# Sliding-window attention and a routed expert layer: loads that wait for units, logits of superchunk 3 from loaded turned values, and routing begun two units sooner

## The chip, the cores and the metric

The kernel runs on one core of a Trainium2 chip. The metric is the device time of the whole kernel in microseconds (us), the median of several runs. Five engines work beside each other, each through its own queue of instructions in order: TensorE (PE, with its weight loads as PEld), VectorE (DVE), ScalarE (ACT), GpSimd (POOL) and SyncE (SP), which here only issues DMAs. They wait for each other by semaphores.

## What is computed

First causal attention with a window of 64 keys, for 8 batches, 8 heads, 576 positions and 64 numbers per head; then, on its output as 4608 rows of 512, a router and eight experts:

```python
scores = scale * np.matmul(q, k.transpose(0, 1, 3, 2))
mask = (rel >= 0) & (rel < window)                      # window = 64
attn = exp(scores - max) / sum                          # per row, under the mask
x = (attn @ v) as (B, S, H * D)
...
logits = np.einsum('bsd,de->bse', x, w_gate)
local_gate = sigmoid(x @ w_local)
e = argmax(logits[b, s]) if s == 0 or local_gate[b, s] < 0.5 else prev_e
h = np.maximum(x[b, s] @ w1[e], 0.0)
out[b, s] = softmax(logits[b, s])[e] * (h @ w2[e])
```

All is in float32. The choice of expert goes along a batch's positions, since a row may take over the expert of the row before.

## The kernel before

**Attention** (function `attention`) takes the 4608 rows in nine superchunks (`sc`, 512 rows each) and each superchunk in four units (`hp`, a pair of heads). A unit's `scores` multiply keys and queries into two banks, ACT takes the exponential into `p` (L416), and VectorE multiplies by the mask (L421), save in the seven units of `BIASED`, where TensorE adds a bias instead. Its `values` (L431) multiply `p` with the values, in two arrangements of the same 512 rows: `va` as loaded and `vb` shifted by half a chunk, which `shift` copies from `va` on ACT and POOL (L360 to L367). A column of ones in the values gives the sum; VectorE takes the reciprocal into `allr` (L436) and multiplies x by it (L441). Scores run two units ahead of values (`LEAD`). After a superchunk POOL writes x to memory (`xs`, L536).

**The gate's logits** come in two ways. For the superchunks in `GATED` (4 to 8) the values turned to columns are loaded (`vtt`), `gates` multiplies them by the gate's weights, and `spread` puts the nine products per head beside the values (`v4`, 74 columns per head in place of 65 in `v3`), so that attention's own product gives the logits (`g`, L439, added up at L534). For the others, 0 to 3, x itself is turned on TensorE in two halves (`turn`, L302, copied by ACT at L305), multiplied and turned back (`gates`, `logits`, L338). The last 64 rows ahead of the first gated superchunk need products too: `gates_ahead` and `back_ahead`.

**Routing** of the first 1728 rows (`Router.first`, `gate`, `places`, `table`) runs beside attention: a generator that is asked for its next piece twice per unit (`step`), each piece saying how long the next should pause, and whether the next one waits for a TensorE result. It begins in unit (4,2), after the logits of superchunk 3. Its end is a table of row numbers by which POOL gathers the first expert's rows.

**Loads.** The queues of TensorE, ACT and SP go in the order of the code; VectorE and POOL are ordered by a scheduler. All loads are issued by SP. Keys and queries of a superchunk (`kq`, 2 MB) lie in a ring of four buffers, v has three buffers and the turned values one. SP issues a load as soon as its buffer is free. Only four times does SP wait for more: `until` issues a copy of one number, and SP waits for that number before it goes on. The first expert's weights, w1 and w2 in four pieces each, go through the same ring.

After attention come the experts: blocks of rows, each two products with an expert's weights, while a second routing for the other rows goes beside the first three. Nothing is changed there.

Of the kernel before, what the change touches and what calls it, by code (L numbers as in the profile page):

```python
# [19 lines left out]
P = 128  # L20
# [22 lines left out]
FB = 3  # L43
# [24 lines left out]
VW = VX + E + 1  # L68
GATED = range(4, NSC)
BIASED = [(4, 3), (5, 1), (5, 3), (6, 0), (6, 1), (6, 2), (6, 3)]  # L70
# [97 lines left out]
def attention(ctx, tc, ring, kq, v3, v4, vt, vh, xs, lt, ok, wg, wg2, ident, rt, ex):  # L168
# [65 lines left out]

    late = cp.tile([1, 4], F32, name="late")

# [113 lines left out]
    def back_ahead():  # L350
        o = bank()[:WIN, :P]
        nc.tensor.transpose(o, ahead, ident)
        nc.scalar.copy(ahead_t[WIN:], o.rearrange("p (h g) -> p h g", h=H)[:, :, :E + 1])

# [69 lines left out]
    def values(sc, hp, p, x, g):  # L424
        va, vb, n = vas[sc], vbs[sc], width(sc)
        xo = pair()
        for s in range(4):
            for j in range(2):
                for par, w in enumerate((vb, va)):
                    b = 2 * s + par  # L430
                    nc.tensor.matmul(xo[par * WIN:(par + 1) * WIN, j, s * VW:s * VW + n],  # L431
                                     lhsT=p[:, j, b * WIN:(b + 1) * WIN], rhs=w[:, s, 2 * hp + j, :n],
                                     start=True, stop=True)
# [7 lines left out]
        nc.vector.tensor_tensor(x[:, :, hp].rearrange("p c j d -> p j c d"), o[:, :, :, :DH],  # L441
                                rr.to_broadcast([P, 2, 4, DH]), op=Alu.mult)

    units = [(sc, hp) for sc in range(NSC) for hp in range(HP)]
    ps = {}
# [25 lines left out]
    for i, (sc, hp) in enumerate(units):  # L471
# [7 lines left out]
        if hp == (0 if sc else 3) and sc + 1 < NSC:  # L479
            moves = shift(sc + 1)  # L480
        for _ in range(2 if sc else 4):
            next(moves, None) if moves else None

        if hp == 3 and sc + 1 in GATED:
            spread(sc + 1, gated)
        elif (sc, hp) == (1, 3):
            gates_ahead()
        elif (sc, hp) == (2, 3):
            back_ahead()
# [27 lines left out]
        if hp == 2 and sc + 1 in GATED:  # L517
            gated = gates(sc + 1)
        if 0 < sc < NSC - 2 and hp == 0:
            load(sc + 2, [whole])  # L520
        if 0 < sc < NSC - 3 and hp == 1:
            load(sc + 3, pairs)
        if hp == 2 and sc + 2 in GATED:
            load(sc + 2, ["turned"])
        if (sc, hp) == (NSC - 3, 3):
            ex.jobs = [ex.weights({}, -1, ("w1",), lambda: until(2, allr[:1, sc, hp, 0, :1]))]
# [175 lines left out]
class Router:  # L702
# [9 lines left out]
    def __init__(self, ctx, tc, lt, xs, tabs, ident):  # L712
        self.nc, self.lt, self.xs, self.tabs, self.ident = tc.nc, lt, xs, tabs, ident
        self.pool = ctx.enter_context(tc.tile_pool(name="rt", bufs=1))
        self.tc, self.behind, self.links = tc, None, []
# [58 lines left out]
    def gate(self, part, psum):  # L774
# [85 lines left out]
        sums = tl("sums", P, 2 * E * CMAX)[:, :2 * n * E]  # L860
        vec.tensor_copy(sums, both)
        pre, tot = sums[:, :n * E], sums[:, n * E:]
# [8 lines left out]
        cnt = self.cnt[part]  # L871
        vec.tensor_tensor(cnt, run[:, :, n - 1], base[:, :, 0], op=Alu.subtract)
        start = tl("start", P, E)
        vec.tensor_copy(start, base[:, :, 0])
        if part:
# [69 lines left out]
    def table(self, psum, cs, ns, lo, hi, idx, gx):  # L945
# [5 lines left out]
        for k in range(0, len(pieces), 2):  # L951
            built = []
            for b, m in pieces[k:k + 2]:
                rowh = self.oh_p.tile([P, PIECE, P], BF16, name="rowh")[:, :m]
                if ns == FIRST:
                    sh = [P, m, P]
                    vec.tensor_tensor(rowh, self.io128.to_broadcast(sh), last(lo[:, b:b + m]).to_broadcast(sh),
                                      op=Alu.is_equal)
                    yield 0.15 * m, False
                one = self.oh_p.tile([P, PIECE, ns], BF16, name="one")[:, :m]  # L960
# [33 lines left out]
    def first(self, psum):  # L994
# [3 lines left out]
        nf = tl("nf", P, E)  # L998
        self.shifted(nf, self.cnt[0], 0, BIG.bit_length() - 1)
        fend = tl("fend", P, E)  # L1000
# [8 lines left out]
        yield 1.8, False  # L1009
        self.experts_of(tabs["ej1"], FB, [(FB, fend)])  # L1010

        CE = [P, C1, E]
        pl = tl("pl", P, CV, E)[:, :C1]
        rank = self.rank[:, :C1]
        vec.tensor_tensor(pl, rank, mid(self.lim1).to_broadcast(CE), op=Alu.is_ge)
        vec.scalar_tensor_tensor(pl, pl, float(2 * N), rank, Alu.mult, Alu.add)
        yield 1.2, False
        vec.tensor_tensor(pl, pl, mid(foff).to_broadcast(CE), op=Alu.add)
        vec.tensor_tensor(pl, pl, self.oh[:, :C1], op=Alu.mult)
        lo, hi = self.places(pl, C1)  # L1020

        vec.tensor_tensor(rank, rank, mid(self.lim1).to_broadcast(CE), op=Alu.subtract)
        yield 2.5, False
        self.weigh(0)
        yield from self.table(psum, slice(0, C1), FIRST, lo, hi, tabs["idx1"], tabs["gx1"])

    def second(self, psum):
# [72 lines left out]
        vec.tensor_tensor(pl, pl, plh, op=Alu.add)  # L1100
        vec.tensor_scalar(none, self.rank[:, :C1], 0.0, float(2 * N), Alu.is_lt, Alu.mult)
        vec.tensor_tensor(pl[:, :C1], pl[:, :C1], none, op=Alu.add)
# [28 lines left out]
class Experts:  # L1131
# [38 lines left out]
    def weights(self, st, n, names=("w1", "w2"), behind=lambda: None):  # L1170
        ej, at = (self.tabs["ej1"], -1 - n) if n < 0 else (self.tabs["ej"], n)
        e = self.nc.values_load(ej[0:1, at:at + 1], engines=[ET.SP], min_val=0, max_val=E - 1,
                                skip_runtime_bounds_check_because="a count of experts, at most E - 1")
        behind()
        for name, w, a, b in (("w1", self.w1, DK, F), ("w2", self.w2, FK, D)):
            if name not in names:
# [6 lines left out]
            st[name] = t.rearrange("p (a b) -> p a b", a=a)  # L1183
        return st

    def begin(self):
# [432 lines left out]
```

## Time and profile before

| what | us |
| --- | --- |
| median of 3 runs (641.36 to 642.15) | 641.81 |
| the profiled execution's own time | 642.1 |
| its span, first to last instruction | 640.0 |
| TensorE busy | 615.6 |
| VectorE busy | 402.3 |
| last value matmul of attention ends | 133.5 |

A stretch is given as start:end in microseconds of the span. A wait in square brackets is the idle time of the engine just ahead of the instruction, and what ended it; "issue" means that nothing in the profile did. A clock of 1.00 is TensorE's full clock. "L431" is line 431 of the kernel before; an x and a number is a count. A float32 matmul of the program is two matmuls, each with a weight load, in the trace.

### The profile page before, as it was taken

Reading aid. Unit: us, or ns where it says so; the run is one execution under the profiler, and the core shown is the slowest. Engines: PE = TensorE matmul, PEld = TensorE weight load, DVE = VectorE, ACT = ScalarE, POOL = GpSimd, SP = SyncE. Lnnn points to the kernel's source line nnn. Section 1 sums busy time; section 2 is a strip of 40 time slices with the busy share of each in tenths; the row PEclk is TensorE's granted clock in tenths of the full one; section 3 lists DMA queues with packets and bytes.
Section 4 is the critical chain, followed back from the end, with each engine's and each line's share of the span. In section 5 each row is a group of like instructions: output and inputs, shape, how many; then the busy total and the mean of one; then the engine's idle time right before and its main releaser. Section 6 shows DMA issues by size and latency. Waiting matters only on the chain. (4 is left out here: it accounts for less than half of the span.)

```text
span 640.0 us, 14994 instructions
## 1 busy us (share of the span) xinstructions
PE 615.6 (96%) x6367; PEld 544.2 (85%) x6367; DVE 402.3 (63%) x752; ACT 200.6 (31%) x368; POOL 133.1 (21%) x132
## 2 busy tenths in 40 slices
PE   8889998899999999999999999999999999999995
PEld 7777777788889999978997999887997998899994
DVE  6676588879968775273654683362917752886730
ACT  3766765612572122113120312021211221213120
POOL 5422112430103202120302120211312022111101
PEclk9999998999999999999999999999999999999998
DMA  9999996969757645786958665769768556956501
GB/s 338 416 418 406 385 366 241 348 236 337 237 171 246 244 166 198 242 316 236 387 189 291 218 234 212 259 235 367 263 228 324 185 199 232 379 167 225 209 17 38
DMA packets 29318, 166.43 MB, mean 260 GB/s; under 512 B 8451, under 2 KB 9497, under 8 KB 20026
## 3 DMA queue, kind: packets, MB, share of 16 engines
q1 hardware_dynamic: 20394, 135.54, 58.4%
q0 software_dynamic: 8848, 29.85, 12.2%
q8 instruction: 52, 0.85, 0.5%
q14 instruction: 24, 0.20, 0.1%
HBM read 146.18 MB, written 19.59 MB: 259 GB/s over the span
## 5 line engine op out<-in xcount | busy, mean ns | idle before, releaser
L1394 POOL DMA_INDIRECT out_dram<-y,idx x36 | 41.1, 1141 | 339.1 <-DVE y L1327 196.5
L1318 PE MATMUL hp<-ws,hs 128*128 128x256 f32 x384 | 88.7, 380 | 0.0
L1318 PEld LDWEIGHTS hp<-ws,hs 128*128 128x128 f32 x384 | 72.6, 190 | 10.5 <-issue 0.8
L1268 PE MATMUL hp<-xs,ws 128*128 128x128 f32 x672 | 79.6, 275 | 0.0
L1268 PEld LDWEIGHTS hp<-xs,ws 128*128 128x128 f32 x672 | 77.3, 192 | 0.0
L1327 DVE SCALAR_TENSOR_TENSOR y<-hp,xg,kept 128x256 f32<-128x256 f32 x48 | 22.6, 482 | 74.2 <-issue 47.0
L1414 PE MATMUL hp<-xt,w 128*64 128x64 f32 (+2 forms) x640 | 66.2, 276 | 0.0
L1414 PEld LDWEIGHTS hp<-xt,w 128*128 128x128 f32 (+1 forms) x640 | 60.8, 170 | 4.1 <-issue 0.7
L1318 PE MATMUL hp<-w,h 128*128 128x256 f32 x256 | 61.1, 382 | 0.0
L1162 POOL DMA_INDIRECT xg<-xs,gx x40 | 50.3, 1258 | 45.6 <-issue 37.4
L1279 DVE TENSOR_TENSOR h<-hp,keep 128x512 f32<-128x512 f32 x42 | 28.6, 690 | 48.1 <-PE hp L1268 48.0
L1268 PEld LDWEIGHTS hp<-xt,w 128*128 128x128 f32 x448 | 53.2, 192 | 2.7 <-issue 1.3
L1268 PE MATMUL hp<-xt,w 128*128 128x128 f32 x448 | 54.7, 275 | 0.0
L1318 PEld LDWEIGHTS hp<-w,h 128*128 128x128 f32 x256 | 47.2, 190 | 6.3 <-issue 0.4
L431 PE MATMUL xo<-vb,p 128*64 128x74 f32 (+1 forms) x576 | 44.5, 230 | 7.0 <-issue 2.9
L416 ACT ACTIVATE p<-sp 128x512 f32<-128x512 f32 x72 | 39.2, 595 | 38.0 <-PE sp L385 35.9
L385 PEld LDWEIGHTS sp<-w 64*64 64x64 f32 x1296 | 38.7, 138 | 12.1 <-issue 8.5
L421 DVE TENSOR_TENSOR p<-p,mask 128x1024 f32<-128x1024 f32 x29 | 36.1, 1245 | 19.5 <-ACT p L416 19.3
L431 PEld LDWEIGHTS xo<-vb,p 128*64 128x64 f32 x576 | 38.9, 138 | 9.9 <-issue 4.4
L385 PE MATMUL sp<-w 64*64 64x128 f32 (+1 forms) x1296 | 43.8, 270 | 2.6 <-issue 1.5
L431 PE MATMUL xo<-va,p 128*64 128x74 f32 (+1 forms) x576 | 44.5, 230 | 1.2 <-issue 1.2
L1280 ACT ACTIVATE h<-h 128x512 f32<-128x512 f32 x42 | 26.3, 630 | 59.1 <-DVE h L1279 59.1
(280 smaller groups left out, 955.0 us busy)
## 6 DMA issues: line engine op xcount, KB each, us to landing
w<-in_w_dram SPq DMA_DIRECT2D x42, 2048.0 KB, 9.2
w<-in_kq_dram SPq DMA_DIRECT2D x17, 1024.0 KB, 8.7
w<-in_w_dram SPq DMA_DIRECT2D x24, 512.0 KB, 9.3
xs<-x POOLq DMA_DIRECT2D x9, 1024.0 KB, 9.5
va<-in_v_dram SPq DMA_DIRECT2D x5, 1184.0 KB, 8.9
vtt<-in_vt_dram SPq DMA_DIRECT2D x5, 1024.0 KB, 7.2
va<-in_v_dram SPq DMA_DIRECT2D x3, 1040.0 KB, 12.2
va<-in_v_dram SPq DMA_DIRECT2D x2, 520.0 KB, 6.8
```

Source lines behind the costliest of these rows:

```text
L385: nc.tensor.matmul(sp[j][c * WIN:(c + 1) * WIN, a:b], lhsT=kt[h, hp, block * WIN:(block + 1) * WIN], rhs=qt[h, hp, a:b], start=not biased, ...
L416: nc.scalar.activation(p[:, j], sp[j], Act.Exp, scale=DH ** -0.5)
L421: masked.append(nc.vector.tensor_tensor(p, p, m.to_broadcast([P, 2, SC]), op=Alu.mult))
L431: nc.tensor.matmul(xo[par * WIN:(par + 1) * WIN, j, s * VW:s * VW + n], lhsT=p[:, j, b * WIN:(b + 1) * WIN], rhs=w[:, s, 2 * hp + j, :n], ...
L1162: asked = self.nc.gpsimd.indirect_dma_start(out=x, out_offset=None, in_=self.xs[:rows, :], in_offset=bass.IndirectOffsetOnAxis(ap=gx[:, s: ...
L1268: nc.tensor.matmul(out[:, m, :], lhsT=a[:, kk, m * P:(m + 1) * P], rhs=b[:, kk, :], start=start and m + kk == 0, stop=stop and (m, kk) == ...
L1279: nc.vector.tensor_tensor(o, x, y, op=add)
L1280: nc.scalar.activation(o, x if y is None else o, Act.Relu)
L1318: nc.tensor.matmul(out, lhsT=a[:, m, :], rhs=b[:, m, :], start=start and m == 0, stop=stop and m == FK // 2 - 1, skip_group_check=True)
L1327: nc.vector.scalar_tensor_tensor(y[i][:, j * w:(j + 1) * w], x, pw[i], y2, Alu.mult, Alu.add)
L1394: self.nc.gpsimd.indirect_dma_start(out=self.out[:, :], out_offset=bass.IndirectOffsetOnAxis(ap=st["idx"][:, s:s + 1], axis=0), in_=y, in_ ...
L1414: nc.tensor.matmul(hp[a, i, :], lhsT=st["w1"][:, kk, m * P:(m + 1) * P][:, a], rhs=st["xt"][:, kk, :n], start=(kk == 0), stop=(kk == DK - 1))
```

## The change

Three things are changed.

*Superchunk 3 is gated*: `GATED` begins at 3. Its x is no longer turned, its turned values are loaded (1 MB), and its v has 74 columns per head.

*Loads wait for units.* In every unit but the first of a superchunk (and in some later ones), `until` makes SP wait for the unit's reciprocals, and then one or two loads are issued: v of two superchunks ahead after `hp` 1 (before: after `hp` 0), the turned values and a quarter of k and q of three ahead after 2, the other three quarters after 3. The first expert's weights go piece by piece, one per unit, from (6,3) on (`piece`). At the start v and k, q of superchunks 2 and 3 are spread over units 0 to 3.

*Routing* begins in unit (4,0). Many of its operations on VectorE are held behind the latest normalisation of x (`rt.after`), the comparison that makes `rowh` is cut in pieces of five chunks, a pause is longer, and one more rule keeps pieces that wait for TensorE out of a superchunk's second half. Apart from that, at the start of a superchunk that follows an ungated one, the copy of the second turn stands ahead of the shift's copies on ACT; two small copies go from ACT to VectorE; and one small operation (`none`) of the second routing is held behind attention.

```diff
-GATED = range(4, NSC)
+GATED = range(3, NSC)
...
-        nc.scalar.copy(ahead, r[:, :WIN])
+        nc.vector.tensor_copy(ahead, r[:, :WIN])
...
-        for _ in range(2 if sc else 4):
-            next(moves, None) if moves else None
+        late_moves = hp == 0 and sc and sc - 1 not in GATED
+
+        def move():
+            for _ in range(2 if sc else 4):
+                next(moves, None) if moves else None
+
+        if not late_moves:
+            move()
...
+        if late_moves:
+            move()
-        if side is None and 4 * sc >= C1 and hp >= 2:
+        if side is None and 4 * sc >= C1:
             side = rt.first(bank)
...
             until(1, allr[:1, 0, 0, 0, :1])
-            load(2, [pairs[0], whole, pairs[1]])
+            load(2, [pairs[0]])
             nc.sync.dma_start(out=vhs, in_=vh)
-            load(3, pairs)
...
-        if 0 < sc < NSC - 2 and hp == 0:
+        if 0 < i < HP * (NSC - 2) and hp:
+            until(2 + i, allr[:1, sc, hp, 0, :1])
+        if i in (1, 2):
+            load(2, [(whole, pairs[1])[i - 1]])
+        if 0 < sc < NSC - 2 and hp == 1:
             load(sc + 2, [whole])
-        if 0 < sc < NSC - 3 and hp == 1:
-            load(sc + 3, pairs)
         if hp == 2 and sc + 2 in GATED:
             load(sc + 2, ["turned"])
+        if sc < NSC - 3 and hp == 2 and sc:
+            load(sc + 3, [slice(0, 1)])
+        if sc < NSC - 3 and hp == 3:
+            load(sc + 3, [slice(1, 2), pairs[1]] if sc else pairs)
...
-        step(not (hp == 2 and sc + 1 in GATED))
-        if (sc, hp) == (NSC - 2, 1):
-            ex.weights(ex.jobs[0], -1, ("w2",), lambda: until(3, allr[:1, sc, hp, 0, :1]))
+        step(not (hp >= 2 and sc + 1 in GATED))
+        at = i - (len(units) - 2 * HP)
+        if 0 <= at < 2 * HP and at != HP - 1:
+            until(2 + i, allr[:1, sc, hp, 0, :1])
+            ex.piece(ex.jobs[0], "w1" if at < HP else "w2", at % HP + (at < HP))
...
+    def after(self, part=0):
+
+        return self.tc.issue_after(self.norm.ins) if self.norm and not part else nullcontext()
...
-        yield 1.5, True
+        yield 1.5 if part else 2.4, True
...
-                    vec.tensor_tensor(rowh, self.io128.to_broadcast(sh), last(lo[:, b:b + m]).to_broadcast(sh),
-                                      op=Alu.is_equal)
-                    yield 0.15 * m, False
+                    for c in range(0, m, PIECE // 2):
+                        d = min(c + PIECE // 2, m)
+                        sh = [P, d - c, P]
+                        with self.after():
+                            vec.tensor_tensor(rowh[:, c:d], self.io128.to_broadcast(sh),
+                                              last(lo[:, b + c:b + d]).to_broadcast(sh), op=Alu.is_equal)
+                        yield 0.15 * (d - c), False
...
+    def piece(self, st, name, i):
+        w, a, b = (self.w1, DK, F) if name == "w1" else (self.w2, FK, D)
+        if not i:
+            t = self.ring.tile([P, a * b], F32, name="w")
+            st[name] = t.rearrange("p (a b) -> p a b", a=a)
+        m = a // PARTS
+        src = w[bass.ds(st["e"], 1)].rearrange("o p (a b) -> (o p) a b", a=a)
+        self.nc.sync.dma_start(out=st[name][:, i * m:(i + 1) * m], in_=src[:, i * m:(i + 1) * m])
```

In the order of instructions this shows at three places. On SP, before, from the load of superchunk 3's k and q on (`w` is k and q, `va` the values, `vtt` the turned ones):

```order
L233 DMA w<-in_kq_dram 128x2048 x2
L228 DMA va<-in_v_dram 128x2080
L233 DMA w<-in_kq_dram 128x2048 x2
L228 DMA va<-in_v_dram 128x2368
L233 DMA w<-in_kq_dram 128x2048 x2
L223 DMA vtt<-in_vt_dram 128x2048
```

And with the change, from the same load to the turned values two superchunks on (`late` is the one-number copy that waits for a unit's reciprocals in `allr`):

```order
L233 DMA w<-in_kq_dram 128x2048 x2
L240 DMA late<-allr 1x1
L228 DMA va<-in_v_dram 128x2368
L240 DMA late<-allr 1x1
L223 DMA vtt<-in_vt_dram 128x2048
L233 DMA w<-in_kq_dram 128x1024
L240 DMA late<-allr 1x1
L233 DMA w<-in_kq_dram 128x1024
L233 DMA w<-in_kq_dram 128x2048
L240 DMA late<-allr 1x1
L228 DMA va<-in_v_dram 128x2368
```

A wait for a unit now stands ahead of each group of loads, and the turned values and wide v come one superchunk sooner. On VectorE, before, where the routing makes `rowh` in superchunk 6 (L436 and L441 are a unit's reciprocal and normalisation):

```order
L928 CAST lo<-lo_i 128x14
L929 CAST hi<-plc_i 128x14
L957 TENSOR_TENSOR rowh<-io_755,lo 128x1280
L436 RECIPROCAL allr<-xo 128x8
L962 TENSOR_TENSOR one<-ios,hi 128x60
L439 TENSOR_TENSOR g<-xo,allr 128x2x4x9
L441 TENSOR_TENSOR x<-xo,allr 128x2x4x64
```

And with the change (`rowh` in the first piece of five chunks, L422 is the product with the mask):

```order
L437 RECIPROCAL allr<-xo 128x8
L440 TENSOR_TENSOR g<-xo,allr 128x2x4x9
L442 TENSOR_TENSOR x<-xo,allr 128x2x4x64
L983 TENSOR_TENSOR rowh<-io_764,lo 128x640
L422 TENSOR_TENSOR p<-p,mask_222 128x1024
L437 RECIPROCAL allr<-xo 128x8
L440 TENSOR_TENSOR g<-xo,allr 128x2x4x9
L442 TENSOR_TENSOR x<-xo,allr 128x2x4x64
L983 TENSOR_TENSOR rowh<-io_764,lo 128x640
```

Each piece of `rowh` moved behind a normalisation. On ACT, before, at the start of superchunk 2 (L305 copies a turn, L360 and L363 are the shift's copies):

```order
L305 COPY p<-xo 128x1024
L416 ACTIVATE p<-sp 128x512 x2
L360 COPY vb<-va 64x520
L363 COPY vb<-va 64x1040
L305 COPY p<-xo 128x1024
```

And with the change:

```order
L306 COPY p<-xo 128x1024
L417 ACTIVATE p<-sp 128x512 x2
L306 COPY p<-xo 128x1024
L361 COPY vb<-va 64x8x65
L364 COPY vb<-va 64x1184
```

The second turn's copy moved ahead of the two copies of the shift.

More of the change, by code (lines that the diff above doesn't have):

```diff
@@ L233, in load @@
                 nc.sync.dma_start(out=kqs[sc][:, part], in_=kq[sc, :, part])
-    late = cp.tile([1, 4], F32, name="late")
+    units = [(sc, hp) for sc in range(NSC) for hp in range(HP)]
+    late = cp.tile([1, 2 + len(units)], F32, name="late")
     def until(i, x):
@@ L352, in back_ahead @@
         nc.tensor.transpose(o, ahead, ident)
-        nc.scalar.copy(ahead_t[WIN:], o.rearrange("p (h g) -> p h g", h=H)[:, :, :E + 1])
+        nc.vector.tensor_copy(ahead_t[WIN:], o.rearrange("p (h g) -> p h g", h=H)[:, :, :E + 1])
     def shift(sc):
@@ L440, in values @@
                                     rr.to_broadcast([P, 2, 4, E + 1]), op=Alu.mult)
-        nc.vector.tensor_tensor(x[:, :, hp].rearrange("p c j d -> p j c d"), o[:, :, :, :DH],
-                                rr.to_broadcast([P, 2, 4, DH]), op=Alu.mult)
-    units = [(sc, hp) for sc in range(NSC) for hp in range(HP)]
+        rt.norm = nc.vector.tensor_tensor(x[:, :, hp].rearrange("p c j d -> p j c d"), o[:, :, :, :DH],
+                                          rr.to_broadcast([P, 2, 4, DH]), op=Alu.mult)
     ps = {}
@@ L480, in attention @@
             moves = shift(sc + 1)
[L481 to L482 removed]
+        late_moves = hp == 0 and sc and sc - 1 not in GATED
[4 more added lines that the diff above has]
+            move()
         if hp == 3 and sc + 1 in GATED:
             spread(sc + 1, gated)
[L486 removed]
+        elif (sc, hp) == (1, 1):
             gates_ahead()
[L488 removed]
+        elif (sc, hp) == (2, 1):
             back_ahead()
@@ L714, in __init__ @@
         self.pool = ctx.enter_context(tc.tile_pool(name="rt", bufs=1))
-        self.tc, self.behind, self.links = tc, None, []
+        self.tc, self.behind, self.links, self.norm = tc, None, [], None
         self.rows_of(ctx, tc, "rt_oh1")
@@ L860, in gate @@
         sums = tl("sums", P, 2 * E * CMAX)[:, :2 * n * E]
-        vec.tensor_copy(sums, both)
+        with self.after(part):
+            vec.tensor_copy(sums, both)
         pre, tot = sums[:, :n * E], sums[:, n * E:]
@@ L871, in gate @@
         cnt = self.cnt[part]
-        vec.tensor_tensor(cnt, run[:, :, n - 1], base[:, :, 0], op=Alu.subtract)
         start = tl("start", P, E)
-        vec.tensor_copy(start, base[:, :, 0])
+        with self.after(part):
+            vec.tensor_tensor(cnt, run[:, :, n - 1], base[:, :, 0], op=Alu.subtract)
+            vec.tensor_copy(start, base[:, :, 0])
         if part:
@@ L998, in first @@
         nf = tl("nf", P, E)
-        self.shifted(nf, self.cnt[0], 0, BIG.bit_length() - 1)
+        with self.after():
+            self.shifted(nf, self.cnt[0], 0, BIG.bit_length() - 1)
         fend = tl("fend", P, E)
@@ L1014, in first @@
         rank = self.rank[:, :C1]
-        vec.tensor_tensor(pl, rank, mid(self.lim1).to_broadcast(CE), op=Alu.is_ge)
-        vec.scalar_tensor_tensor(pl, pl, float(2 * N), rank, Alu.mult, Alu.add)
+        with self.after():
+            self.experts_of(tabs["ej1"], FB, [(FB, fend)])
+            vec.tensor_tensor(pl, rank, mid(self.lim1).to_broadcast(CE), op=Alu.is_ge)
+            vec.scalar_tensor_tensor(pl, pl, float(2 * N), rank, Alu.mult, Alu.add)
         yield 1.2, False
[L1018 to L1023, printed above, removed]
+        with self.after():
+            vec.tensor_tensor(pl, pl, mid(foff).to_broadcast(CE), op=Alu.add)
+            vec.tensor_tensor(pl, pl, self.oh[:, :C1], op=Alu.mult)
+        yield 0.8, False
+        with self.after():
+            lo, hi = self.places(pl, C1)
+            vec.tensor_tensor(rank, rank, mid(self.lim1).to_broadcast(CE), op=Alu.subtract)
+        yield 1.7, False
         self.weigh(0)
@@ L1100, in second @@
         vec.tensor_tensor(pl, pl, plh, op=Alu.add)
-        vec.tensor_scalar(none, self.rank[:, :C1], 0.0, float(2 * N), Alu.is_lt, Alu.mult)
+        with self.after():
+            vec.tensor_scalar(none, self.rank[:, :C1], 0.0, float(2 * N), Alu.is_lt, Alu.mult)
         vec.tensor_tensor(pl[:, :C1], pl[:, :C1], none, op=Alu.add)
@@ L1174, in weights @@
         behind()
+        st["e"] = e
         for name, w, a, b in (("w1", self.w1, DK, F), ("w2", self.w2, FK, D)):
```

4 lines of the change are left out of this document (2 added, 2 removed).

## The prediction

> **What bounds the kernel now.** I read the page first, for the shares of the engines.
>
> ```profile
> PE 615.6 (96%) x6367; PEld 544.2 (85%) x6367; DVE 402.3 (63%) x752; ACT 200.6 (31%) x368; POOL 133.1 (21%) x132
> ```
>
> TensorE is the bound of the whole, and an average of 96% leaves 24 us. Where they lie is told by the busy times by stage, here cut at the first value matmul of superchunks 1 to 8 and at the end of attention (columns: stretch, its length, then busy time and count of PE, weight load, DVE, ACT, POOL; granted clock, DMA share, GB/s).
>
> ```profile
> 25.56:41.12 15.56, 13.40 (x309) 10.90 (x308) 8.90 (x14) 9.60 (x16) 6.52 (x6) 1.00 1.02 416
> 41.12:54.81 13.69, 13.01 (x302) 10.75 (x302) 11.39 (x36) 8.87 (x15) 2.84 (x4) 1.00 1.02 415
> 54.81:69.28 14.47, 13.65 (x313) 10.86 (x312) 8.54 (x13) 10.78 (x19) 3.46 (x5) 1.00 0.99 386
> 69.28:84.70 15.42, 13.34 (x313) 9.99 (x313) 10.28 (x30) 10.42 (x20) 4.03 (x5) 1.00 0.99 385
> 84.70:97.13 12.43, 12.39 (x315) 10.22 (x315) 10.81 (x47) 7.27 (x13) 0.99 (x1) 1.00 1.00 369
> 97.13:111.99 14.86, 12.35 (x294) 10.47 (x290) 12.12 (x35) 8.42 (x15) 2.93 (x4) 0.89 0.66 230
> 111.99:124.72 12.73, 11.54 (x305) 9.62 (x299) 10.94 (x25) 8.42 (x15) 6.04 (x5) 1.00 1.01 333
> 124.72:133.48 8.76, 7.01 (x179) 6.44 (x173) 6.17 (x13) 3.24 (x6) 0.81 (x1) 1.00 0.88 344
> 133.48:640.00 506.52, 498.14 (x3628) 446.31 (x3628) 306.19 (x515) 119.98 (x232) 92.65 (x79) 1.00 0.65 233
> ```
>
> After attention TensorE idles 8.4 of 506.5 us and the change touches nothing there but one small operation, so every microsecond taken from attention is one off the end. Attention has two parts: to the end of superchunk 5 the DMA engines are full (share 0.99 to 1.02) and TensorE nearly so (65.8 of 71.6 us); from superchunk 6 the DMA is not full at first, and TensorE still loses time and even clock (0.89). TensorE's waits up to 134 us say to whom:
>
> ```profile
> PE xo L431 <- issue: 4.1, 4, 1.8
> PE xo L431 <- DVE x L441: 2.5, 1, 2.5
> PE xo L431 <- ACT p L305: 1.5, 3, 0.8
> PE sp L385 <- issue: 1.5, 2, 1.1
> PE r L822 <- DVE loc L817: 0.9, 1, 0.9
> PE xo L302 <- ACT p L305: 0.8, 1, 0.8
> PE r L812 <- ACT va L348: 0.6, 1, 0.6
> ```
>
> No wait names a load. The largest, "issue", is a wait for nothing that the profile names. Three of its places in TensorE's timeline, and the matmuls counted up to just ahead of each:
>
> ```profile
> 33.91 0.27 PE L431 MATMUL xo<-vb,p 128*64 128x65 f32 x1 [0.65 <-issue]
> ...
> 122.94 0.22 PE L431 MATMUL xo<-va,p 128*64 128x74 f32 x1 [1.19 <-issue]
> ...
> 129.11 0.22 PE L431 MATMUL xo<-vb,p 128*64 128x74 f32 x1 [1.75 <-issue]
> ```
>
> ```profile
> 2.00:33.80 31.80, 28.07 (x604) 24.28 (x604) 21.67 (x35) 18.37 (x30) 15.60 (x24) 1.00 1.01 401
> ...
> 2.00:122.80 120.80, 108.69 (x2513) 89.86 (x2514) 88.41 (x220) 76.25 (x130) 38.64 (x47) 0.99 0.96 368
> 2.00:129.00 127.00, 113.11 (x2640) 93.89 (x2641) 93.14 (x229) 78.42 (x134) 39.45 (x48) 0.99 0.97 370
> ```
>
> They lie in the middle of a unit, where the code waits for nothing, and 127 matmuls apart (2640 less 2513; 2513 less 604 is 15 times 127). The page's queue of instructions explains that number:
>
> ```profile
> q8 instruction: 52, 0.85, 0.5%
> ```
>
> 52 packets of 16 KB for 6367 matmuls and 6367 weight loads are 245 instructions each, or some 123 pairs. So TensorE stops where the next packet of its own program has not come: it moves on the same DMA engines as the loads, and comes late when these are full. From 122.94 to 129.11, 6.2 us, is then the time of one packet, while 127 pairs take 4.8 us of work in superchunk 7 (11.54 for 305).
>
> **The change part by part.** All against the profiled execution, span 640.0 and own time 642.1; the median of the runs, 641.8, is 0.3 less, and what I take off one I take off the other. A measurement of this kernel tells about 0.2% (1.3 us) from no change.
>
> *A, routing behind x's normalisation.* The 2.5 us wait is in superchunk 6:
>
> ```profile
> 99.66 1.49 DVE L957 TENSOR_TENSOR rowh<-io,lo 128x1280 bf16<-128x1280 f32 x1
> ...
> 101.45 0.68 DVE L441 TENSOR_TENSOR x<-xo,allr 128x512 f32<-128x512 f32 x1
> ```
>
> ```profile
> 102.18 0.28 PE L431 MATMUL xo<-vb,p 128*64 128x74 f32 x1 [2.52 <-DVE x L441]
> ...
> 103.98 1.99 PE L385 MATMUL sp<-w 64*64 64x128 f32 x36
> ...
> 108.13 1.12 PE L385 MATMUL sp<-w 64*64 64x128 f32 x36
> ```
>
> VectorE was in the routing's comparison of 1.49 us, with others queued ahead of it, when unit (6,0)'s values were ready, and TensorE waited for x's normalisation; then it ran at a lower clock, so the next scores took 1.99 instead of 1.12. The comparison is now cut in pieces of five chunks and it and its neighbours are held behind a normalisation. That removes 2.5, and of the clock 0.9 in these scores and, by the same ratio 1.99 to 1.12 over about one unit's values, some 0.6 more: 4.0.
>
> *B, superchunk 3 from loaded turned values.* Two turns go, and its values get 74 columns for 65. The first row groups the turns, eight of them, 1.1 us each; the others are one unit's values with 65 and with 74 columns (columns: PE, weight load, clock, DMA).
>
> ```profile
> L302 PE MATMUL xo<-ident,x 128*128 128x128 f32 x64 | 8.8, 278 | 1.1 <-ACT p L305 0.8 <-issue 0.3
> ```
>
> ```profile
> 61.50:62.70 1.20, 1.15 (x32) 1.01 (x32) 1.00 1.00 413
> 76.15:77.45 1.30, 1.25 (x32) 1.10 (x32) 1.00 1.03 425
> ```
>
> 2 x 1.1 less 4 x 0.10 is 1.8 us off TensorE. The gate products and the turning back stay as many. ACT loses two copies and gains three small ones, VectorE gains five small operations; both have spare time there (8.5 to 11.4 busy of 13.7 to 15.6), so nothing.
>
> *C, the copy of a turn ahead of the shift's copies.* Of the waits for ACT's p, the 1.5 us at values are those where this order is wrong or the turn is gone. The 0.8 at the first turn stays, since superchunk 0's order is kept. 1.5 off. The two small copies moved from ACT to VectorE are hidden.
>
> *D, routing two units sooner.* Its transposes made TensorE wait 0.9 and 0.6. The longer pause after the scan, and no step of that kind in the second half of a superchunk, bear on both; it can save none or all of 1.5. I take 0.5, since the chain through VectorE stays. Its end and the gathers behind it come sooner, which nobody waits for.
>
> *E, loads unit by unit.* It sets a one-number copy that waits for a unit's reciprocals ahead of each load, and cuts k and q. Of "issue" (4.1 and 1.5) the two late places are 2.9, the early ones 2.7. Late, four pieces of w1 and four of w2 (512 KB each) now come one to a unit, so the packet finds a short queue: 2.9 off. Early, the loads still fill the engines: nothing off (bound 2.7 off; or as much on again, where TensorE now runs pages faster). [...]
>
> *F, more bytes.* The sizes, from the issues:
>
> ```profile
> va<-in_v_dram SPq DMA_DIRECT2D x5, 1184.0 KB, 8.9
> vtt<-in_vt_dram SPq DMA_DIRECT2D x5, 1024.0 KB, 7.2
> ...
> va<-in_v_dram SPq DMA_DIRECT2D x3, 1040.0 KB, 12.2
> ```
>
> 1024 KB plus 144 KB is 1.2 MB, at the 416 to 386 GB/s of superchunks 1 to 3 2.9 to 3.1 us of a full DMA. It costs all of it if the DMA sets the pace up to superchunk 5, nothing if the free third of superchunk 6 (about 5 us) takes it up. The stretches are nearer to full, so I take three quarters, 2.3.
>
> The sum: 4.0 + 1.8 + 1.5 + 0.5 + 2.9 - 2.3 = 8.4 off, 633.7 for the profiled execution, **633.4** for the median. What is late next is the DMA: A and E lie after the full part and come off whole, B, C and D inside it.
>
> **The rivals.** *The DMA keeps its pace.* Up to superchunk 5 the share is already 1, so B, C and D only turn into waits of TensorE for packets and loads, and F is paid whole: 4.0 + 2.9 - 3.1 = 3.8 off, 638.0. For it: the shares. Against it: no wait of before is for a load.
>
> *Values come too late, slower.* Each v is now asked for a unit later, behind that unit's reciprocals.
>
> ```profile
> 37.95 0.33 SPq L228 DMA_DIRECT2D va<-in_v_dram  x1
> ```
>
> ```profile
> 52.88 1.16 POOL L361 COPY vb<-va 64x1184 f32<-64x1184 f32 x1 [8.37 <-PE xo L431]
> ```
>
> From issue to first use were 14.9 us; a unit takes 3.4 (13.7 for four), which leaves 11.5, and v lands in 8.9 to 12.2. If it lands later, ACT's copies of the shift stand ahead of the next exponentials and hold TensorE, in six superchunks. At 14 us that is 6 x 2.5 = 15.0 against 8.4 saved: 6.6 slower, 648.4. It decides from 12.9 us on (6 x 1.4). For it: a full DMA. Against it: the queue ahead of each v is shorter by the same rule. [...]
>
> *It doesn't do what it says.* VectorE has as much to do (12.1 of 14.9 us in superchunk 6), so the wait of A comes back at the masks' products, and the packets still come late because bytes, not their order, fill the engines. Left are B and C less F: 1.8 + 1.5 - 3.1 = 0.2 off, 641.6.
>
> **How the numbers follow.** The forecast gets 0.62, the DMA's pace 0.20, values too late 0.10, no effect 0.08. The first two are faster (0.82), the last is within 0.2%, the third slower. The range goes down to 628.5: F hidden (2.3) and the early pages gone too (2.7) would be 628.4. It goes up to 640.0, which holds the DMA's pace with two of E's three microseconds kept, and leaves out the two last cases, 0.18.
>
> **What would show it.** Right: attention's last values matmul ends 7 to 10 us sooner than 133.5; no wait for x's normalisation over 1 us and a clock of 1.00 all through; no "issue" wait from superchunk 6 on; a DMA share of 1 that lasts longer, past superchunk 5. The DMA's pace: superchunks 1 to 5 together stay at 71 us or more, with new waits for "issue". Wrong: waits of ACT or POOL for va that TensorE then shows at scores or values, or a stretch behind attention longer than 506.5 us.

## The result, and the profile after

The change made the kernel slower.

| | before | after |
| --- | --- | --- |
| median, us (6 runs each) | 642.14 | 646.49 |
| lowest to highest | 641.36 to 644.29 | 646.06 to 647.56 |
| ratio of the times, 95% interval | | 1.0058 [1.0041, 1.0076] |
| profiled execution: own time, span | 642.1, 640.0 | 647.56, 645.3 |
| last value matmul of attention ends | 133.48 | 138.25 |

The two medians lie 4.35 us apart, a quotient of 1.0068; the ratio that goes with the interval is smaller, 3.7 us, and the gains and costs of the experiments below are taken from such ratios.

First the busy times of the kernel after, cut at the end of attention as before (stretch, length, then busy time and count of PE, weight load, DVE, ACT, POOL; clock, DMA share, GB/s).

```profile
2.00:138.25 136.25, 118.81 (x2724) 97.45 (x2724) 100.25 (x241) 78.42 (x135) 41.00 (x48) 0.96 0.95 353
138.25:645.30 507.05, 498.24 (x3628) 446.56 (x3628) 306.27 (x516) 119.98 (x232) 93.00 (x79) 1.00 0.64 236
```

and attention of the kernel before, cut in the same way:

```profile
2.00:133.48 131.48, 117.48 (x2740) 97.93 (x2740) 95.61 (x235) 79.49 (x136) 39.45 (x48) 0.99 0.96 367
```

The stretch behind attention is as long as before (507.05 for 506.52). Attention is 4.8 us longer, with a clock of 0.96. Of that TensorE is busy only 1.3 longer (118.81 for 117.48), and that at a lower clock; the rest is waiting. For whom it waits, up to 150 us:

```profile
PE xo L432 <- issue: 5.1, 4, 2.7
PE r L316 <- DVE ahead_t L354: 3.2, 1, 3.2
PE r L832 <- DVE vk L825: 2.9, 1, 2.9
...
PE sp L386 <- issue: 2.3, 3, 1.4
PE r L865 <- DVE ex L857: 0.8, 1, 0.8
```

The wait of 2.5 for x, on which the forecast had taken 4.0, is gone but for 0.2. Three others have come: one on `ahead_t`, one on `vk`, and one of 2.7 for nothing named. In TensorE's timeline each is followed by slow work:

```profile
47.13 1.93 PE L316 MATMUL r<-p,wgs 128*32 128x512 f32 x8 [3.24 <-DVE ahead_t L354]
48.99 1.62 PE L386 MATMUL sp<-w 64*64 64x128 f32 x36
...
77.11 0.39 PE L832 MATMUL r<-ident,vk 128*14 128x128 f32 x2 [2.86 <-DVE vk L825]
79.60 1.67 PE L386 MATMUL sp<-w 64*64 64x128 f32 x36
...
111.73 0.28 PE L432 MATMUL xo<-vb,p 128*64 128x74 f32 x1 [2.72 <-issue]
...
114.28 1.41 PE L386 MATMUL sp<-w 64*64 64x128 f32 x36
```

A unit's 36 matmuls of scores took 1.12 us at a granted clock of 1.00 (108.13 before), here 1.62, 1.67 and 1.41 at clocks of 0.66, 0.64 and 0.76. A superchunk's length, from VectorE's last reciprocal of one to that of the next, shows where it went: superchunk 2 takes 19.9 for 15.0, superchunk 4 15.7 for 14.2, superchunks 5 and 6 together 31.5 for 30.0; the others gain 3 together.

**The first wait** is for a copy that the forecast called hidden. VectorE's timeline ahead of it:

```profile
43.44 0.63 DVE L783 CAST ios<-ios_i 128x54 f32<-128x54 int32 x1
...
45.51 1.14 DVE L290 TENSOR_SCALAR bias<-p,rowf 128x256 bf16<-128x256 f32 x4
46.57 0.25 DVE L292 TENSOR_SCALAR unit<-p,rowf 128x64 bf16<-128x64 f32 x1
46.85 0.23 DVE L354 COPY ahead_t<-r 64x72 f32<-64x72 f32 x1
```

The copy (0.23) stands behind the tables that VectorE makes for the routing and the biases. In unit (2,1), to which the change moved `back_ahead`, the gate products of superchunk 1 (L316) need the same bank `r` right behind it.

**The second** is the first step of the routing, which now begins while POOL copies the shift:

```profile
72.01 1.17 POOL L362 COPY vb<-va 64x1184 f32<-64x1184 f32 x1 [12.07 <-DMA va<-in_v_dram]
73.12 1.30 POOL L366 COPY vb<-va 64x1184 f32<-64x1184 f32 x1
...
87.94 1.17 POOL L362 COPY vb<-va 64x1184 f32<-64x1184 f32 x1 [12.81 <-DMA va<-in_v_dram]
```

```profile
73.31 1.23 DVE L817 TENSOR_TENSOR eq<-lt,mx 128x112 f32<-128x112 f32 x1
...
74.77 1.22 DVE L422 TENSOR_TENSOR p<-p,mask 128x1024 f32<-128x1024 f32 x1
...
76.90 0.16 DVE L825 SCALAR_TENSOR_TENSOR vk<-own,fresh 128x14 f32<-128x14 f32 x1
```

and the same comparison in the kernel before, away from POOL's copies:

```profile
78.21 0.27 DVE L797 TENSOR_TENSOR eq<-lt,mx 128x112 f32<-128x112 f32 x1
```

The comparison took 1.23 for 0.27 and ended 0.12 behind POOL's copy. The mask's product and x's normalisation stood in the queue between it and `vk`, while TensorE's transposes of `vk` stand ahead of the values. The slow comparison is the smaller part: in four of the runs below that begin the routing in the same unit (a4, c1, c2, e3) it took 0.26, and TensorE still waited 1.6 to 2.1 for `vk`. The POOL rows also show what the second rival looked for: 43.6 us of idle time ahead of its copies at L362 ended with a landing of `va`, five times; in the kernel before it was 2.9, once.

### The profile page after: what moved, and what is told of

It is laid out like the page before. It is cut to its first block, busy times and chain, and to the rows that moved or that the text cites. A ratio compares the mean times of both kernels' runs of the same rounds, so it can differ in the third digit from the quotient of the medians.

```text
span 645.3 us, 15027 instructions
## 1 busy us (share of the span) xinstructions
PE 617.1 (96%) x6351; PEld 544.0 (84%) x6351; DVE 407.0 (63%) x759; ACT 199.6 (31%) x367; POOL 135.0 (21%) x132
## 5 line engine op out<-in xcount | busy, mean ns | idle before, releaser
L432 PE MATMUL xo<-vb,p 128*64 128x74 f32 (+1 forms) x576 | 45.8, 232 | 4.6 <-issue 4.4
L422 DVE TENSOR_TENSOR p<-p,mask 128x1024 f32<-128x1024 f32 x29 | 37.5, 1294 | 18.8 <-ACT p L417 18.5
L432 PE MATMUL xo<-va,p 128*64 128x74 f32 (+1 forms) x576 | 46.0, 232 | 0.8 <-issue 0.7
L1271 DVE TENSOR_TENSOR ws<-w 128x1024 f32<-128x1024 f32 x32 | 39.0, 1221 | 9.6 <-PE hp L1358 7.0
```

What stands on the lines that cost most here:

```text
L422: masked.append(nc.vector.tensor_tensor(p, p, m.to_broadcast([P, 2, SC]), op=Alu.mult))
L1271: self.nc.vector.tensor_tensor(o, x, y, op=sub)
```

## The experiments

Ratios are to the kernel before on the same chip, with their 95% interval; single executions of one kernel lie 1.5 to 12 us apart here, so what a profile shows is where time goes, and how much is told by the ratios.

**Who copies, and where it stands.** Theory: the copy's place on VectorE costs what the first wait shows. Rival: it is the routing that costs.

```diff
-        nc.vector.tensor_copy(ahead_t[WIN:], ...)       # a1: the change, with this copy on ACT
+        nc.scalar.copy(ahead_t[WIN:], ...)
```

> The changed kernel with the copy of ahead_t back on ACT. First theory (two small steps that VectorE must do first hold TensorE, 3.2 us at the copy of ahead_t and 2.9 us at vk, each with a slow clock behind it): the wait of 3.2 us and some 1.3 us of slow clock go, 4.5 us less than the changed kernel, about 642.0. Rival (the loads set the pace, so that a wait taken away comes back as waits for packets or data): at most 1 us less, about 645.5.

1.0039 [1.0018, 1.0060]. The wait was still there, and now for ACT:

```profile
PE r L832 <- DVE vk L825: 2.3, 1, 2.3
PE r L316 <- ACT ahead_t L354: 2.0, 1, 2.0
```

The wait is 2.0 for 3.2, and the two ratios' intervals overlap, so who copies is a part at most. Then the place, in a unit where no gate products follow:

```diff
-        elif (sc, hp) == (2, 1):       # b1: the change, back_ahead elsewhere
+        elif (sc, hp) == (1, 3):
             back_ahead()
```

> The changed kernel with ahead turned back in unit (1,3) and not in (2,1). Theory (one bank: in (2,1) the gate products of superchunk 1 need the bank that holds ahead, and must wait for whoever copies it, ACT or VectorE): the wait of 3.2 us and the slow clock behind it go, 4.5 us less than the changed kernel, so a ratio to before of about 0.999 where the changed kernel had 1.006. Rival (VectorE's preparation at (2,0) holds up whatever comes next, or the loads' pace takes it): less than 1.5 us, 1.0035 or more.

1.0002 [0.9974, 1.0029]: 0.56% less than the whole change, 3.6 us, with the copy still on VectorE and its products two units earlier. The wait for `ahead_t` is gone from the profile, the one for `vk` is not. What cost is the place: in (2,1) the copy stands behind other work on either engine, and the bank's next user stands right behind it. The move takes both away, so no run tells them apart.

**The routing's start.**

```diff
-        if side is None and 4 * sc >= C1:                  # a2: the change; a3: a1 with the same
+        if side is None and 4 * sc >= C1 and hp >= 2:
```

> The changed kernel with routing begun in unit (4,2) again, all else as changed. First theory: the wait of 2.9 us for vk and some 1.5 us of slow clock go and nothing comes in their place, since x's normalisation still goes first: about 642.1. Rival of the loads' pace: about 645.5. A third way: routing two units later puts its later steps on superchunk 6 and brings back the 2.5 us wait there: about 646.

> The changed kernel with both: the copy of ahead_t on ACT, and routing begun in unit (4,2). First theory: both savings add, about 637.6, and TensorE's clock is 1.00 up to superchunk 5. Rival of the loads' pace: no less than 644.5.

1.0160 [1.0135, 1.0185] and 1.0144 [1.0117, 1.0170], both against what was expected. TensorE's waits of a2 from 100 us on:

```profile
PE tp L1236 <- DMA xg<-xs,gx: 5.3, 2, 4.1
PE xo L432 <- issue: 3.2, 2, 3.0
PE xo L432 <- DVE x L442: 2.1, 2, 1.8
```

The routing that pauses longer ends later, and begun in (4,2) its table comes too late: TensorE, in whose queue the first expert's rows stand ahead of attention's last unit, waits 4.1 us for them at 137.7. So the early start is the price of the slower routing. The fair comparison takes both back, on top of b1:

```diff
-        if side is None and 4 * sc >= C1:                  # d1
+        if side is None and 4 * sc >= C1 and hp >= 2:
...
-        yield 1.5 if part else 2.4, True
+        yield 1.5, True
...
-        step(not (hp >= 2 and sc + 1 in GATED))
+        step(not (hp == 2 and sc + 1 in GATED))
```

> The change with its turned-back products in (1,3) (1.0002 of before), and the routing begun in (4,2) with the short pause and the old rule for steps, as before; the holding behind x's normalisation stays. Theory 1, the early start costs TensorE the waits for vk and ex (2.3 and 1.9 us) and nothing is won by it: these waits shrink to under 1 each and the ratio falls to 0.993 to 0.998. Theory 2, what the early start takes at vk and ex it gives back at the end of attention: other waits (x, packets) come in their place and the ratio stays at 0.998 to 1.003.

1.0015 [0.9984, 1.0046], so nothing that can be told from b1: theory 2. The waits for `vk` and `ex` are indeed gone, those for packets are larger:

```profile
PE xo L432 <- issue: 9.1, 6, 2.4
PE sp L386 <- issue: 3.0, 3, 1.5
...
PE r L842 <- DVE loc L837: 0.9, 1, 0.9
```

This execution took 6.6 us more than the median of its runs, so the size of the rows is not that of a usual run.

**The loads.** First the change with attention's loads as before, then before with the change's loads alone.

```diff
-            load(2, [pairs[0]])                            # a4: the change
+            load(2, [pairs[0], whole, pairs[1]])
+            load(3, pairs)
...
-            until(2 + i, allr[:1, sc, hp, 0, :1])
...
-        if 0 < sc < NSC - 2 and hp == 1:
+        if 0 < sc < NSC - 2 and hp == 0:
             load(sc + 2, [whole])
+        if 0 < sc < NSC - 3 and hp == 1:
+            load(sc + 3, pairs)
```

> The changed kernel with attention's loads issued as before, as soon as buffers are free (the first expert's weights still piece by piece). First theory: both VectorE waits stay, and the order of the loads is worth little: 645.5 to 648. Rival: what the waiting loads cost comes back, 642.5 or less.

> The kernel before with only the order of loads changed (attention's loads and the first expert's weights wait for units; superchunk 3 and routing as before). Term E of the prediction: 2.9 us less, a ratio of 0.9955. Rival (the packets of instructions come as late, since bytes fill the engines, and a later issue makes some later): 0 to 3 us more, 1.000 to 1.005.

a4 1.0019 [0.9995, 1.0043], b3 1.0056 [1.0034, 1.0078]. The loads alone make the kernel before slower by 3.6 us; without attention's part of them the change is 2.5 us better (1.0058 less 1.0019). A stretch early in attention and nearly all of it, in b3 and then in the kernel before:

```profile
40.00:60.00 20.00, 18.76 (x445) 15.28 (x449) 16.33 (x42) 14.92 (x23) 7.53 (x9) 1.00 0.89 344
2.00:140.00 138.00, 123.43 (x2756) 103.10 (x2757) 102.37 (x247) 79.98 (x137) 39.56 (x49) 0.98 0.93 347
```

```profile
40.00:60.00 20.00, 18.50 (x423) 14.90 (x426) 14.91 (x41) 14.35 (x22) 5.10 (x8) 1.00 1.01 408
2.00:140.00 138.00, 124.00 (x2771) 103.61 (x2772) 101.06 (x256) 80.44 (x138) 42.69 (x52) 0.99 0.94 359
```

The DMA engines are no longer full where they were (0.89 for 1.01), and over the whole stretch they moved less (347 GB/s for 359). In ACT's and TensorE's timelines at superchunk 8's shift:

```profile
117.27 1.18 ACT L364 COPY vb<-va 64x1184 f32<-64x1184 f32 x1 [1.21 <-DMA va<-in_v_dram]
118.47 1.08 ACT L417 ACTIVATE p<-sp 128x512 f32<-128x512 f32 x2
```

```profile
119.82 1.98 PE L386 MATMUL sp<-w 64*64 64x128 f32 x34 [1.38 <-ACT p L417]
```

This is the chain of the rival word for word: v late, the shift's copy waits, the exponentials stand behind it, TensorE waits and then runs slowly. The next two ask for v in unit 0 again, on top of b1 (c1) and of b3 (c3); c2 is b1 with all loads, the weights too, as before.

```diff
-        if 0 < sc < NSC - 2 and hp == 1:                   # c1, c3
+        if 0 < sc < NSC - 2 and hp == 0:
             load(sc + 2, [whole])
```

> The change with its turned-back products in (1,3) (as in the run on the bank, 1.0002 of before), and v of two superchunks ahead asked for in unit 0 again, as in the kernel before; k, q, turned values and weights still come unit by unit. Theory 1, the pacing costs because v comes late: the waits of POOL and ACT for va go, superchunk 8's shift holds no exponentials, and 1.5 to 3 us are won against the run on the bank: 0.995 to 0.998 of before. Theory 2, the pacing costs because the DMA engines stand idle for part of each superchunk and the rest comes later: v is earlier but k, q and turned values are then later, and the time stays at 0.999 to 1.002.

> The kernel before with the change's loads alone (that was 1.0056), and v asked for in unit 0 as before. Theory 1 (v late): the wait of 1.4 us for exponentials behind superchunk 8's shift and the slow scores behind it go, POOL no longer waits for va, ratio 1.000 to 1.003. Theory 2 (idle DMA): ratio stays at 1.004 to 1.007.

> The change with its turned-back products in (1,3) and all loads and weights issued as before: what is left of the change is superchunk 3, the copy order, and the routing. If the loads cost here what they cost on top of before (3.6 us), this is 0.9945 to 0.997 of before, faster than both kernels. If the loads' cost was made up by what they give the routing's end (weights behind the table's rows on SP's queue) it is 0.999 to 1.002.

c1 1.0035 [1.0012, 1.0058], c3 1.0027 [1.0009, 1.0046], c2 1.0018 [0.9997, 1.0040]. On top of before, an earlier v takes back about half of what the loads cost (1.9 of 3.6 us, and the two intervals overlap); on top of b1 it takes back nothing. There all the loads together make no difference that can be told (c2, 1.0018, for b1's 1.0002). In c3 the wait for exponentials behind superchunk 8's shift is still there, against the expectation, though not the slow scores behind it (1.11 for 1.98):

```profile
117.96 1.11 PE L386 MATMUL sp<-w 64*64 64x128 f32 x34 [1.37 <-ACT p L417]
```

But there v was late again. VectorE, SP and ACT in c3:

```profile
99.69 2.41 DVE L965 TENSOR_TENSOR rowh<-io,lo 128x1280 bf16<-128x1280 f32 x1
102.03 0.20 DVE L437 RECIPROCAL allr<-xo 128x8 f32<-128x8 f32 x1
...
102.25 0.59 SPq L240 DMA_DIRECT2D late<-allr  x1
...
103.92 0.33 SPq L228 DMA_DIRECT2D va<-in_v_dram  x1
...
115.06 1.18 ACT L364 COPY vb<-va 64x1184 f32<-64x1184 f32 x1 [0.86 <-DMA va<-in_v_dram]
```

SP still waits for superchunk 5's last reciprocals ahead of this v, for the loads in front of it, and VectorE made them late, behind the routing's comparison; the kernel before issued the same v at 96.11, 4.9 ahead of those reciprocals (101.06). So c3 does not bound what a late v costs, and a load that waits for reciprocals also waits for whatever holds VectorE. Last, the weights alone:

```diff
-            ex.jobs = [ex.weights({}, -1, ("w1",), lambda: until(2, allr[:1, sc, hp, 0, :1]))]    # d2: before
+            ex.jobs = [ex.weights({}, -1, (), lambda: until(2 + i, allr[:1, sc, hp, 0, :1]))]
+            ex.piece(ex.jobs[0], "w1", 0)
...
-            ex.weights(ex.jobs[0], -1, ("w2",), lambda: until(3, allr[:1, sc, hp, 0, :1]))
+        at = i - (len(units) - 2 * HP)
+        if 0 <= at < 2 * HP and at != HP - 1:
+            until(2 + i, allr[:1, sc, hp, 0, :1])
+            ex.piece(ex.jobs[0], "w1" if at < HP else "w2", at % HP + (at < HP))
```

> The kernel before with the first expert's weights in eight pieces, one per unit, and attention's own loads as before. Theory 1, what the loads cost is v and k, q, not the weights: ratio 0.996 to 1.000, with the late waits for nothing named (1.19 and 1.75) smaller. Theory 2, the pieces cost too, since they are issued behind the routing table's transfers on SP and come later: 1.002 to 1.004.

0.9962 [0.9941, 0.9983], 2.4 us faster. From 120 us on one wait for nothing named is left, where before had 1.19 and 1.75:

```profile
126.46 0.22 PE L432 MATMUL xo<-vb,p 128*64 128x74 f32 x1 [0.99 <-issue]
```

So the loads' edit is two edits of opposite sign: the weights win 2.4, and attention's own loads cost the rest when they are added to that, 0.94% or 6.0 us, give or take some 2 (the difference of the two ratios and their intervals).

**Are packets late because the DMA is full?** The kernel before without k and q of superchunks 2 and 3:

```diff
+                if sc in (2, 3):                           # c4: before
+                    kts[sc], qts[sc] = kts[1], qts[1]
+                    continue
                 if sc not in kqs:
```

> The kernel before without the loads of k and q of superchunks 2 and 3, 2 MB each (their scores take superchunk 1's, so x of these rows is another). If packets of TensorE's instructions come late because the loads fill the DMA engines, the waits for nothing named at about 27.7, 33.9 and 39.9 us (0.42, 0.65 and 1.09) shrink to under 0.3 each while the DMA share there is under 0.9; the ones behind superchunk 6 stay. If the waits come from the page's end itself whatever the DMA does, they stay as they are.

One execution, 641.25 us; the scores of these superchunks then take superchunk 1's k and q. TensorE's waits to 140 us, and a stretch, c4 ahead of the kernel before:

```profile
PE xo L434 <- issue: 3.1, 3, 2.0
```

```profile
35.00:40.00 5.00, 4.73 (x112) 4.13 (x110) 3.31 (x4) 3.84 (x7) 2.75 (x3) 1.00 0.54 175
```

```profile
35.00:40.00 5.00, 3.91 (x102) 3.38 (x94) 2.42 (x4) 2.80 (x5) 2.01 (x3) 1.00 1.03 424
```

Of the waits at 27.7, 33.9 and 39.9 (0.42, 0.65 and 1.09) the first two are gone and 0.27 is left of the third, now at 37.81; b5 and d2, which load everything, have all three. The first of the three waits at values is 0.45 at 50.15, the others, 0.65 and 2.03, come behind superchunk 6. This fits late packets: in attention every wait for nothing named, seven in the kernel before and eight in the kernel after, ended 2.4 to 2.7 us after a packet in the page's queue of instructions. The share alone does not make them late: between 25 and 35 it was still 0.99 to 1.02 in c4, and in the kernel before ten such packets came between 41 and 97 us, at a share of 0.99 to 1.02, with one wait, 0.51 at 52.24. That the loads queued ahead make them late is the author's estimate from this one execution.

**Superchunk 3** on top of before, and the same with 2 MB less to load (its scores then take superchunk 2's k and q):

```diff
-GATED = range(4, NSC)                                      # b4: before, with the copy order, the turned-back
+GATED = range(3, NSC)                                      # products in (1,3) and the copies on VectorE
...
+                if sc == 3:                                # d3: b4
+                    kts[sc], qts[sc] = kts[2], qts[2]
+                    continue
```

> The kernel before with only superchunk 3 gated and the second turn's copy ahead of the shift's (ahead turned back in (1,3), where the bank is free; loads as soon as buffers are free; routing as before). Terms B, C and F of the prediction: 1.8 + 1.5 - 2.3, 1.0 us less, a ratio of 0.9985. If the 1.2 MB more are hidden: 3.3 less, 0.995. Rival of the DMA's pace: 0 to 3 us more, 1.000 to 1.005.

> Superchunk 3 gated on top of before (that was 1.0021), but without the load of k and q of superchunk 3 (2 MB; its scores take those of superchunk 2, so x of these rows is another). If what superchunk 3 costs is its 1.2 MB on full DMA engines, taking 2 MB off must turn it round: 0.994 to 0.998, with the waits for nothing named before 60 us gone. If it is the work on the engines, it stays at 1.000 to 1.003.

1.0021 [0.9999, 1.0043] and 1.0011 [0.9985, 1.0037]. Less to load didn't turn it round, and neither ratio can be told from 1: the bytes are not what takes the gain, or a small part of it. b4's waits:

```profile
PE xo L431 <- issue: 7.9, 5, 2.5
...
PE sp L385 <- DMA w<-in_kq_dram: 1.0, 1, 1.0
PE r L325 <- DMA vtt<-in_vh_dram: 1.0, 1, 1.0
```

Superchunk 4, whose first unit had the second turn, takes 12.8 us for 14.2, and 12.5 in d3: the turns' gain is there. But superchunks 5 and 6 together take 2.3 longer, and superchunks 1 and 2 3.6: there the gate products of the last 64 rows, now earlier, wait 1.0 for their load, and the scores and values for packets. Packet waits at values are 7.9 in b4, for 4.1 before, and in d3 they are not back at that:

```profile
PE xo L434 <- issue: 5.8, 4, 1.8
```

Why they grow with fewer bytes, too, is open.

**x's normalisation and the copy order**, one by one on top of before:

```diff
-        vec.tensor_copy(sums, both)                        # b5: before, with all of the change's
+        with self.after(part):                             # holding, and the comparison in pieces
+            vec.tensor_copy(sums, both)
...
+        late_moves = hp == 0 and sc and sc - 1 not in GATED    # d4: b5
...
+        if late_moves:
+            move()
```

> The kernel before with only the routing's operations held behind x's normalisation and the comparison cut in pieces (routing begins in (4,2) and pauses as before). Term A of the prediction: 4.0 us less, a ratio of 0.994. Rival (the wait comes back elsewhere, at the masks or where TensorE waits for the routing): within 1 us of before, 0.9985 to 1.0015.

> The kernel before with routing held behind x's normalisation (that was 0.9994) and with the copy of a second turn ahead of the shift's copies on ACT. If the copy order's gain of 0.5 and 0.8 us at values comes off whole: 0.997 to 0.9985. If in the part where the DMA engines are full every such gain turns into a wait for packets or loads: 0.999 to 1.001.

b5 0.9994 [0.9972, 1.0017], nothing that can be told from before; d4 0.9962 [0.9937, 0.9988]. In b5 the wait for x is gone and a packet is late in the next unit:

```profile
104.99 0.22 PE L431 MATMUL xo<-va,p 128*64 128x74 f32 x1 [1.61 <-issue]
```

So here the gain of superchunk 6 turned into a wait of 1.61. TensorE's waits for a turn's copy at values are still there in b5:

```profile
PE xo L431 <- ACT p L305: 1.7, 4, 0.8
```

In d4 no such row is left, so the copy order does what it should. By the two ratios that is 2.0 us, but their intervals overlap, and only the two edits together (2.4 us) are clear of noise.

**What is worth keeping.** e1 is d4 with d2's weights; e3 is b1 with a4's loads.

> The kernel before with three parts of the change: routing held behind x's normalisation and the copy order (together 0.9962), and the first expert's weights piece by piece (alone 0.9962). Theory 1, these act on different stretches and add up: 0.990 to 0.995. Theory 2, both only empty the same waits of superchunks 6 to 8, or what one wins the other's waits take: 0.995 to 0.998.

> The change with its turned-back products in (1,3) and attention's own loads issued as before, the weights still piece by piece. Theory 1, attention's paced loads are what is left of the cost: the change without both costs is 0.994 to 0.9985 of before. Theory 2, superchunk 3 and the early routing take back what the weights, the order and the normalisation give: 0.999 to 1.002.

e1 640.38 for 645.59, **0.9927 [0.9907, 0.9948]**: faster than both kernels, and the parts add up (0.9962 twice is 0.9924). e3 0.9988 [0.9967, 1.0009]: the change with its two costs mended is at most a little faster than before. On the same chip e1 is 0.61% faster than e3, 3.9 us: what e3 has beyond e1 is superchunk 3, the earlier routing with its longer pause, and the two small copies, for which the forecast had 0.0 (B 1.8 and D 0.5, less F 2.3). e3 and b1 differ by 0.14% only, so attention's loads cost less beside superchunk 3 and the early routing than the 0.94% on top of before; what makes the difference was not found. One candidate that no run tests is c3's: on top of before the routing can hold the reciprocals that the loads wait for, and in b1 and e3 it is itself held behind x's normalisation.

## Why the prediction was wrong

The forecast was 8.4 us faster; it became 3.7 slower by the ratio. In the order of its terms:

- **The bound** was read rightly: all of it lies in attention, the stretch behind is unchanged, and "issue" is late packets, by the queue of instructions (2.4 to 2.7 us from a packet to the end of each wait) and by c4.
- **A**, 4.0: the wait for x went, as foretold, but alone it was worth 0.4, not told from nothing (b5). The step that failed is "A and E lie after the full part and come off whole": a packet 1.61 late stood next in the same superchunk.
- **B less F**, with C: 1.0 was to be won, 1.3 was lost (b4, an interval from nothing to 2.8). B itself shows in superchunk 4, 1.4 us shorter. F, three quarters of 1.2 MB at full rate, was the wrong price: 2 MB less gave back 0.10% (d3), where 2 MB at that rate, 416 to 386 GB/s, would make it some 0.8% (5 us). What the loss in b4 consists of was seen only in part (a wait of 1.0 for the load behind the earlier `gates_ahead`, more late packets).
- **C**, 1.5: the waits went, as foretold; 2.0 by d4 less b5 agrees with it, but is not clear of noise.
- **D**, 0.5: 2.9 and 0.8 of waits came for `vk` and `ex`, since TensorE's steps of the routing, two units earlier in its queue, are ready before VectorE's chain. They cost no more than the late start does (d1), but the slower routing needs the early start (a2, 1.016).
- **E**, 2.9: for the weights right, 2.4 (d2). For attention's loads it was nothing, and was 6.0 the other way on top of before, 2.5 in the change itself (a4), and 0.9, within noise, once the bank was free (e3). The step that failed is the second rival's slack of 11.5 us, which counted one unit. The load of `va` now stands behind the end of unit 1 and no longer at the start of unit 0, two units later. (The same count had v land in 8.9 to 12.2 us; asked for later, it landed within 7.0 here.) SyncE's timeline after shows the issue that belongs to POOL's copy at 72.01:

```profile
65.03 0.33 SPq L228 DMA_DIRECT2D va<-in_v_dram  x1
```

  From there to the copy, which v's landing released, are 7.0 us: the slack is at most that, less than the shortest of those landing times. The rival had the sign and about the size (6.6 slower) with a chance of 0.10. That the size is near is luck: the change's loss goes with `back_ahead` in (2,1) (b1), which no rival named, and v asked for early gave back 1.9 of 3.6 us on top of before (c3) and nothing on top of b1 (c1).
- **"The two small copies are hidden"** failed too, and by itself made nearly all of the change's loss, 3.6 us (b1). The forecast looked at engines with spare time, not at what is queued ahead of the copy and who needs its bank, and it never costed the move of `back_ahead` to (2,1).
- **The sums** come out.

On top of before the parts add to more than the change: loads 3.6, superchunk 3 with the copy order 1.3, the bank 3.6, the normalisation -0.4, together 8.1 for 3.7. The rest is not told apart: the parts share waits, and no run has the early routing without superchunk 3. So what loses the forecast's gain once the bank is free (b1 as slow as before, e3 3.9 us behind e1) stays open between superchunk 3 and the routing.

## What to carry to other kernels

Before calling a small moved operation free, look at what stands ahead of it on its new engine and who needs the buffer that it empties; here the place of a 0.23 us copy cost 3.6. Before holding a load back, ask how soon it is needed: here, at a DMA share of 0.94 (2 to 140 us before), the same rule won 2.4 us with weights for later and lost 6.0, on top of the kernel before, with the next superchunks' operands. When an edit has several parts, time each alone: three of them gave 0.9927, all of them 1.0058.

## What the hardware showed that was not expected

- A VectorE comparison of 112 numbers per partition took 1.23 us in each of the four kernels in which it started inside a POOL copy (after, a1, b1, d1), and ended 0.11 to 0.12 behind that copy; it took 0.26 or 0.27 in all the others.
- After idle times of 2.7 to 3.2 us (after) TensorE's next 36 matmuls of scores took 1.41 to 1.67 us, at a granted clock of 0.76 to 0.64, instead of 1.12 at 1.00, another 0.3 to 0.6 us in these alone. A wait of 2.00 (a1) was followed by the usual 1.12. The wait does not decide it alone: behind 1.38 in b3 34 of them took 1.98, behind 1.37 in c3 1.11.
- TensorE stood up to 2.72 us for nothing named (111.73 after), and 3.35 in e1, at places some multiple of 127 matmuls apart, give or take a few (after: 603, 730 and 2130 from 2 us on stand ahead of the waits at 32.81, 39.10 and 111.73). The last packet in the queue of instructions had come 2.5 us before TensorE went on at 111.73. In e1 it had come between 105 and 106, TensorE went on at 107.88, and the DMA share was 0.62, 0.28, 0.21 and 0.12 in the four microseconds from 104 on, so the DMA was not full while TensorE waited. With fewer bytes loaded (c4) the crossings from 25 to 40 us cost 0.27 in all.
